# Sparse attention followed by a gated feed-forward on one core: fewer fillers and value sums first in the prologue; in unit 0 output products ahead of value products, and the last two pairs of x turned together, the last one copied by VectorE

## The chip, the core and the metric

The kernel runs on one core of a Trainium2 chip. The metric is the device time of one execution in microseconds (us); the median of several executions is quoted. The profile of one execution covers the span from its first to its last instruction, which is about 1.8 us shorter than the time.

## The reference

```python
# attention: q, k, v are [4, 8, 768, 64]
k_sum = k.reshape(B, H, nb, 32, D).max(axis=3)      # one key per block of 32
v_sum = v.reshape(B, H, nb, 32, D).mean(axis=3)     # one value per block
scores = concat(local scores within 16 positions, block scores + log(32))
x = softmax(scores) @ concat(v, v_sum)              # -> [3072, 512]
# gated feed-forward
h = gelu(x @ w_gate) * (x @ w_val)                  # 512 -> 1536
out = x + sigmoid(x @ w_res) * (h @ w_out)
```

## The kernel before

The work is cut into eight units of 384 rows. The heads go in four pairs. For a unit, TensorE makes scores `s`; ScalarE takes the exponential `P`; VectorE masks it; TensorE makes the value products `ao`; VectorE divides by the row sum (`xn`); the result is turned (`xp`, copied to `xT`). Then come twelve weight groups, numbered `fo` 0 to 11, each of one gate group `g` and one value group `vv` (four matmuls each). ScalarE takes gelu of `g`, and VectorE multiplies it by `vv` (`gvT`, called a product here). TensorE writes `g` and `vv` into four buffers of PSUM, its output memory. A later group can only start when ScalarE's gelu or VectorE's product has released its buffer; a semaphore, a counter that one engine raises and another waits for, tells it so. Slack is the time between such a release and the start that needs it. The output stage of a unit makes `r` (residual gate) and `f` (output products from `gvT` and `w_out`), and VectorE makes the residual steps `th` and `o`. The attention of the next unit is woven into this stage.

The first attention has nothing to hide behind; that is the prologue. Fillers (`keep_warm`) are matmuls on zeros whose result nobody reads; they keep TensorE busy.

```python
tq = [turn_pair(q_sb[0], hp, turn_tile(q_sb[0], ps_mm, "mm")) for hp in range(NP)]
for hp in range(3):
    q_place(0, hp, tq[hp])
keep_warm(1)
# ... scores of the four pairs, first value sums ...
vsum_mm(0, vs, 3, 8)
keep_warm(2)
# ...
for hp in range(3):
    av_first(hp, st, ao[hp], 0, BAND)       # own products of pairs 0..2
vsum_mm(0, vs, 8, 11)
av_first(3, st, ao[3], 0, BAND)             # own products of pair 3
vsum_mm(0, vs, 11, NT)
nc.vector.tensor_copy(vblk[...], vs[0][...])   # casts of the value sums
nc.scalar.copy(vblk[...], vs[1][...])
# ...
keep_warm(1)
for hp in range(4):
    av_first(hp, st, ao[hp], BAND, 128)     # products with the value sums
    av_end(hp, st, ao[hp])
keep_warm(3)
xt_step(0, 0, st, **turn[0])                # first turn of x
```

Unit 0's output stage, and two parts of the loop:

```python
def first_out(u, st, gvT, nst):
    # ...
    turn = dict(pool=ps_t, tag="t", copy=nc.scalar.copy)
    s_step(n, 0, nst)
    s_step(n, 1, nst, TO2)
    for sub in range(NSUB):
        res_step(st, sub)
    av_step(n, 0, nst)
    # ... see the diff

# loads, issued by GpSimd, in this order: w_gate and w_val in six chunks each,
# q_sb[1] ahead of the last chunk pair, w_res, then w_out in three chunks
for c in range(6):
    if c:
        load_w(w_gate, wg_src, c)
    load_w(w_val, wv_src, c)
    if c == 4:
        q_sb[1] = load_q(1, QJ)
nc.gpsimd.dma_start(out=w_res[:], in_=...)
for c in range(3):
    ...                                       # w_out

# unit 0: k, v and q of the second batch are asked for
load_k(nb, k_sb[nb], 0, 1)
v_loads(nb)
load_q_nat(nb)
# unit 1, after the weight groups fo = 0, 1, 2, 3: one pair of keys each on VectorE:
# a reduce over the block (L228) and three copies (L232, L236, L237)
if fo < NP:
    k_place(nb, fo, tk[fo])
```

The softmax here doesn't subtract the row's maximum and nothing guards it: scores larger than these inputs give would overflow.

Of the kernel before, what the change touches and what calls it, by code (L numbers as in the profile page):

```python
# [15 lines left out]
def kernel(  # L16
# [21 lines left out]
    FO = DFF // 128  # L38
    QT = 64
    NT = S // QT  # L40
    HT = NT // 2
    TU = S // 2
    NSUB = TU // 128
    NU = 2 * B
    NP = H // 2
    BAND = QT + 2 * WIN
# [14 lines left out]
    ps_o = ctx.enter_context(tc.tile_pool(name="ps_o", bufs=1, space=bass.MemoryType.PSUM))  # L61
# [73 lines left out]
    with tc.manual_schedule():  # L135
# [112 lines left out]
        def q_place(half, hp, tp):  # L248
            qj = q_sb[half].shape[2]
            nc.scalar.copy(qT[0][:, 3 * half:3 * half + 3, hp].rearrange("d c (p j) -> d c p j", j=qj),  # L250
                           tp.rearrange("d j (c p) -> d c p j", c=3))
# [10 lines left out]
        def vsum_mm(b, vs, lo, hi):  # L262
            for t in range(lo, hi):
                for i in range(2):
                    nc.tensor.matmul(vs[i][96:128, 0:DM // 2], bmat[:, t, :],
                                     vext[b % 2][0:QT, t, 4 * i:4 * i + 4, 0:D],
                                     start=(t == 0), stop=(t == NT - 1))
# [59 lines left out]
        def av_step(u, hp, st, pool=ps_o, tag="ao"):  # L327
            b, half = u // 2, u % 2
            P = st["P", hp]
            ao = pool.tile([128, NSUB, 2, D + 1], F32, tag=tag, name="ao")  # L330
            for sub in range(NSUB):
                for hh in range(2):
                    for e in range(2):
                        t = 2 * sub + e
                        nc.tensor.matmul(ao[64 * e:64 * e + 64, sub, hh, :], P[:, hh, t, :],  # L335
                                         vext[b % 2][:, half * HT + t, 2 * hp + hh, 0:D + 1],
                                         start=True, stop=True, skip_group_check=True)
            av_end(hp, st, ao)

        def av_first(hp, st, ao, lo, hi):  # L340
            P = st["P", hp]
            for sub in range(NSUB):
                for hh in range(2):
                    for e in range(2):
                        t, h = 2 * sub + e, 2 * hp + hh
                        rhs = vblk[lo:hi, h, :] if lo else vext[0][0:hi, t, h, 0:D + 1]
                        nc.tensor.matmul(ao[64 * e:64 * e + 64, sub, hh, :], P[lo:hi, hh, t, :], rhs,  # L347
                                         start=(lo == 0 and sub == 0 and hh == 0), stop=(lo > 0),
                                         skip_group_check=True)

        def av_end(hp, st, ao):
            rz = work.tile([128, NSUB, 2, 1], F32, tag="rz", name="rz")
            nc.vector.reciprocal(rz[:], ao[:, :, :, D:D + 1])
            xn = st["xn"][:, hp].rearrange("p s (h d) -> p s h d", d=D)
            nc.vector.tensor_mul(xn, ao[:, :, :, 0:D], rz.to_broadcast([128, NSUB, 2, D]))  # L355

        def xt_step(u, ko, st, pool, tag, copy=nc.vector.tensor_copy):
            xp = pool.tile([128, TU], BF16, tag=tag, name="xp")
            for sub in range(NSUB):
                nc.tensor.transpose(xp[:, sub * 128:(sub + 1) * 128],  # L360
                                    st["xn"][:, ko, sub, :], ident[:])
            copy(st["xT"][:, ko, :], xp[:])
# [5 lines left out]
        def new_unit():  # L368
            return {"xn": upool.tile([128, KO, NSUB, 128], BF16, tag="xn", name="xn"),
                    "xT": upool.tile([128, KO, TU], BF16, tag="xT", name="xT")}  # L370
# [12 lines left out]
        def mm_tile(name):  # L383
            return ps_mm.tile([128, 512], F32, tag="mm", name=name)
# [24 lines left out]
        def res_step(st, sub):  # L409
            ss = slice(sub * 128, (sub + 1) * 128)  # L410
            r = mm_tile("r")
            for ko in range(KO):
                nc.tensor.matmul(r[:], st["xT"][:, ko, ss], w_res[:, ko, :],  # L413
                                 start=(ko == 0), stop=(ko == KO - 1))
            st["th", sub] = work.tile([128, DM], F32, tag="th", name="th")
            nc.scalar.activation(st["th", sub][:], r[:], AF.Tanh, scale=0.5)  # L416

        def ffn_step(st, gvT, sub, lo, hi):
            ss = slice(sub * 128, (sub + 1) * 128)
            if lo == 0:  # L420
                st["f", sub] = mm_tile("f")
            for fo in range(lo, hi):
                nc.tensor.matmul(st["f", sub][:], gvT[:, fo, ss], w_out[:, fo, :],  # L423
                                 start=(fo == 0), stop=(fo == FO - 1), skip_group_check=True)
# [13 lines left out]
        def end_step(u, st, sub):  # L438
            end_part(u, st, sub, st["f", sub], slice(0, DM))
# [12 lines left out]
        def keep_warm(n):  # L452
            wp = ps_s.tile([128, 2, 512], F32, tag="s", name="wp")
            for _ in range(n):
                nc.tensor.matmul(wp[:, 0], warm[:, 0:128], warm[:], start=True, stop=True)  # L455
# [11 lines left out]
        tq = [turn_pair(q_sb[0], hp, turn_tile(q_sb[0], ps_mm, "mm")) for hp in range(NP)]  # L467
        for hp in range(3):
            q_place(0, hp, tq[hp])
        keep_warm(1)  # L470
        st = new_unit()
        vs = [ps_t.tile([128, 512], F32, tag="t", name="vs"), ps_o.tile([128, 512], F32, tag="ao", name="vs")]
        s_step(0, 0, st)
# [5 lines left out]
        s_step(0, 2, st)  # L479
        s_step(0, 3, st, MM2)  # L480
        vsum_mm(0, vs, 3, 8)
        keep_warm(2)
        gvT = upool.tile([128, FO, TU], BF16, tag="gvT", name="gvT")
        ao = [ps_mm.tile([128, NSUB, 2, D + 1], F32, tag="mm", name="ao") for _ in range(NP)]
        for hp in range(3):
            av_first(hp, st, ao[hp], 0, BAND)
        vsum_mm(0, vs, 8, 11)
        av_first(3, st, ao[3], 0, BAND)
        vsum_mm(0, vs, 11, NT)
        nc.vector.tensor_copy(vblk[96:128, 0:H // 2, 0:D],  # L490
                              vs[0][96:128, 0:DM // 2].rearrange("p (h d) -> p h d", d=D))
        nc.scalar.copy(vblk[96:128, H // 2:H, 0:D],
                       vs[1][96:128, 0:DM // 2].rearrange("p (h d) -> p h d", d=D))
        nc.scalar.activation(gate1[:], bias_t[0:1, :], AF.Gelu)
        keep_warm(1)
        for hp in range(4):
            av_first(hp, st, ao[hp], BAND, 128)
            av_end(hp, st, ao[hp])
        keep_warm(3)
        turn = [dict(pool=ps_t, tag="t", copy=nc.scalar.copy), dict(pool=ps_o, tag="ao", copy=nc.scalar.copy)]  # L500
        xt_step(0, 0, st, **turn[0])
        keep_warm(1)
# [39 lines left out]
        def first_out(u, st, gvT, nst):  # L542
            n = u + 1
            other = dict(pool=ps_t, tag="t")
            turn = dict(pool=ps_t, tag="t", copy=nc.scalar.copy)
            s_step(n, 0, nst)
            s_step(n, 1, nst, TO2)
            for sub in range(NSUB):
                res_step(st, sub)
            av_step(n, 0, nst)  # L550
            av_step(n, 1, nst, **other)
            s_step(n, 2, nst)
            for sub in range(NSUB):
                ffn_step(st, gvT, sub, 0, 4)
            xt_step(n, 0, nst, **turn)
            av_step(n, 2, nst)
            s_step(n, 3, nst)
            ffn_step(st, gvT, 0, 4, 8)
            ffn_step(st, gvT, 1, 4, 8)
            xt_step(n, 1, nst, **turn)  # L560
            ffn_step(st, gvT, 2, 4, 8)
            av_step(n, 3, nst)
            xt_step(n, 2, nst, **turn)
            ffn_step(st, gvT, 0, 8, FO)
            end_step(u, st, 0)
            ffn_step(st, gvT, 1, 8, FO)
            xt_step(n, 3, nst, **turn)
            ffn_step(st, gvT, 2, 8, FO)
            end_step(u, st, 1)
            end_step(u, st, 2)  # L570
# [40 lines left out]
        for u in range(NU):  # L611
# [7 lines left out]
            if u:  # L619
                gvT = upool.tile([128, FO, TU], BF16, tag="gvT", name="gvT")  # L620
# [42 lines left out]
            if u == NU - 1:  # L663
                last_out(u, st, gvT)
            else:
                nst = new_unit()
                (mid_out if u else first_out)(u, st, gvT, nst)
                st = nst
# [30 lines left out]
```

## Time and profile before

| | before |
|---|---|
| time, median of 3 | 257.49 us (257.44 to 257.61) |
| span of the profiled run | 255.7 us |
| TensorE busy | 97% |
| first matmul of unit 1 | 52.82 us |

From the page of the kernel before: the busy line, the TensorE clock and the DMA rate in forty slices of 6.4 us, and the chain of waits by engine.

```profile
PE 247.6 (97%) x2279; PEld 138.7 (54%) x2304; DVE 157.5 (62%) x349; ACT 127.4 (50%) x213; POOL 110.5 (43%) x155
...
PEclk9999999999999999999999999999999999999999
...
GB/s 80 178 142 174 197 202 207 189 167 164 134 40 87 169 114 140 126 142 169 131 11 94 174 110 157 108 150 154 130 15 73 141 0 3 50 138 0 0 3 123
...
PE 91%; ACT 3%; DMA 2%; DVE 2%; issue 1%; POOLq 0%; DVEq 0%
```

TensorE is busy all through, at full clock, and 91% of the chain that ended last is TensorE's. Slices five to eight (26 to 51 us) move about 200 GB/s: the weights are still coming in while unit 0 computes.

The timeline of TensorE in the prologue of before. Columns: start, length, engine, line, operation, output and inputs, active rows and columns, shape, count, and in brackets the idle time before and what ended it.

```profile
11.75 0.39 PE L455 MATMUL wp<-warm 128*128 128x512 bf16 x1
12.20 0.48 PE L292 MATMUL s<-ident,mneg 128*128 128x384 bf16 x2
...
16.20 0.39 PE L455 MATMUL wp<-warm 128*128 128x512 bf16 x1
16.74 0.76 PE L347 MATMUL ao<-vext,P 96*64 96x65 bf16 x36
...
18.49 0.39 PE L265 MATMUL vs<-vext,bmat 64*32 64x256 bf16 x2
...
19.30 0.95 PE L347 MATMUL ao<-vblk,P 32*64 32x65 bf16 x48
...
20.84 0.33 PE L360 MATMUL xp<-ident,xn 128*128 128x128 bf16 x3
```

A filler sits before the scores (12.20) and before the own products (16.74); the last value sums (18.49) stand behind pair 3's own products; the first turn is at 20.84.

TensorE late in unit 0 of before:

```profile
36.22 0.82 PE L375 MATMUL g<-xT,w_gate 128*128 128x384 bf16 x4
36.88 0.81 PE L375 MATMUL vv<-xT,w_val 128*128 128x384 bf16 x4
...
39.38 0.39 PE L413 MATMUL r<-w_res,xT 128*128 128x512 bf16 x1
```

No wait precedes these. A landing is the moment at which a transfer's completion reaches its semaphore in the trace. In this trace the last `w_val` chunk landed at 36.53, 0.35 us ahead of its use at 36.88, and `w_res` at 39.08, 0.30 us ahead of its use at 39.38.

VectorE where unit 0 ends and unit 1 begins (the seam), before:

```profile
50.30 0.56 DVE L355 TENSOR_TENSOR xn<-ao,rz 128x384 bf16<-128x384 f32 x1
51.13 0.69 DVE L429 SCALAR_TENSOR_TENSOR th<-th,f 128x512 f32<-128x512 f32 x1 [0.27 <-PE f L423]
...
55.11 0.55 DVE L381 TENSOR_TENSOR gvT<-ge,vv 128x384 bf16<-128x384 f32 x1
55.96 0.95 DVE L228 TENSOR_REDUCE ks<-kW 128x24 bf16<-128x768 bf16 x1 [0.30 <-ACT kW L243]
...
57.11 0.19 DVE L236 COPY kW<-kW 128x176 bf16<-128x176 bf16 x1
57.22 0.19 DVE L237 COPY kW<-kW 128x176 bf16<-128x176 bf16 x1
57.33 0.54 DVE L381 TENSOR_TENSOR gvT<-ge,vv 128x384 bf16<-128x384 f32 x1
```

```profile
54.44 5.31 POOL L123 DMA_DIRECT2D q_nat<-in_q_dram  x6
```

From 51.13 on VectorE runs with one rest of 0.30 us until 63.8: six residual steps, then products and key pairs in turn. TensorE meanwhile, before:

```profile
52.82 0.81 PE L375 MATMUL g<-xT,w_gate 128*128 128x384 bf16 x4
...
58.31 0.81 PE L375 MATMUL g<-xT,w_gate 128*128 128x384 bf16 x4
58.96 0.81 PE L375 MATMUL vv<-xT,w_val 128*128 128x384 bf16 x4
...
61.56 0.81 PE L375 MATMUL vv<-xT,w_val 128*128 128x384 bf16 x4
```

The groups follow each other at 0.65 us, without a gap.

### The profile page before, as it was taken

To read this page: it belongs to the slowest core of one execution; us is meant where nothing else is said; L and a number is where in the kernel's file an instruction comes from. 1 tells how busy PE (TensorE), PEld (TensorE's weight loads), DVE (VectorE), ACT (ScalarE), POOL (GpSimd) and SP (SyncE) were. 2 spreads that over 40 slices of the span, in tenths; PEclk is the share of its full clock that TensorE was granted. 3 is DMA by queue.
4 is the path that set the end of the run, shared out by engine and by line. 5 is a ranking of instruction groups with operands and counts; after the bars stand their busy time and mean duration, and the time that the engine had idled before them with its cause. 6 is when DMAs were issued, how large, how long until landed. Compare 5 with 4: busy or idle time off the path is not lost.

```text
span 255.7 us, 5810 instructions
## 1 busy us (share of the span) xinstructions
PE 247.6 (97%) x2279; PEld 138.7 (54%) x2304; DVE 157.5 (62%) x349; ACT 127.4 (50%) x213; POOL 110.5 (43%) x155
## 2 busy tenths in 40 slices
PE   7999999999999999999999999999999999999994
PEld 2566664565654565546654565545554565455544
DVE  5965776399367544767567544857567544854424
ACT  6666359366493338344482338244482337253320
POOL 8897542193334988265405986256404000000000
PEclk9999999999999999999999999999999999999999
DMA  5999999999923999979703999979803500240003
GB/s 80 178 142 174 197 202 207 189 167 164 134 40 87 169 114 140 126 142 169 131 11 94 174 110 157 108 150 154 130 15 73 141 0 3 50 138 0 0 3 123
DMA packets 98475, 29.34 MB, mean 115 GB/s; under 512 B 83592, under 2 KB 95312, under 8 KB 98352
## 3 DMA queue, kind: packets, MB, share of 16 engines
q0 software_dynamic: 68720, 14.76, 69.8%
q1 hardware_dynamic: 29728, 14.21, 25.6%
q8 instruction: 18, 0.29, 0.5%
q14 instruction: 9, 0.07, 0.2%
HBM read 29.36 MB, written 6.29 MB: 139 GB/s over the span
## 4 chain that ended last, share of the span: by engine, by line
PE 91%; ACT 3%; DMA 2%; DVE 2%; issue 1%; POOLq 0%; DVEq 0%
PE g L375 25%; PE vv L375 24%; PE f L423 23%; PE r L413 7%; PE ao L335 3%; PE s L299 2%; DMA k_sb<-in_k_dram 2%; PE tp L211 2%; PE wp L455 1%; ACT P L317 1%; PE vs L273 1%; PE ao L347 1%; ACT P L314 1%; DVE o L432 1%; DVE th L429 1%
## 5 line engine op out<-in xcount | busy, mean ns | idle before, releaser
L381 DVE TENSOR_TENSOR gvT<-ge,vv 128x384 bf16<-128x384 f32 x96 | 52.7, 552 | 51.2 <-PE vv L375 46.8
L380 ACT ACTIVATE ge<-g 128x384 f32<-128x384 f32 x96 | 47.0, 491 | 68.5 <-DVE gvT L381 38.0
L375 PE MATMUL g<-xT,w_gate 128*128 128x384 bf16 x384 | 78.8, 326 | 0.2
L375 PE MATMUL vv<-xT,w_val 128*128 128x384 bf16 x384 | 78.7, 326 | 0.0
L423 PE MATMUL f<-w_out,gvT 128*128 128x512 bf16 x262 | 62.7, 379 | 1.3 <-issue 1.0
L375 PEld LDWEIGHTS <-w_gate 128*128 128x128 bf16 x384 | 37.2, 98 | 26.5 <-issue 1.6
L375 PEld LDWEIGHTS <-w_val 128*128 128x128 bf16 x384 | 37.5, 98 | 24.8 <-issue 0.3
L423 PEld LDWEIGHTS <-gvT 128*128 128x128 bf16 x276 | 25.7, 98 | 29.2
L103 POOL DMA_DIRECT2D vext<-in_v_dram x48 | 33.0, 730 | 13.8 <-DMA w_out<-in_moe_w_out_dram 5.6
L416 ACT ACTIVATE th<-r 128x512 f32<-128x512 f32 x24 | 13.5, 607 | 27.5 <-PE r L413 27.5
L429 DVE SCALAR_TENSOR_TENSOR th<-th,f 128x512 f32<-128x512 f32 (+2 forms) x26 | 16.7, 641 | 14.2 <-PE f L423 14.2
L321 DVE TENSOR_TENSOR P<-P,maskt 128x768 bf16<-128x768 bf16 x30 | 16.9, 562 | 12.1 <-ACT P L317 6.6
L285 POOL COPY vext<-vsum 32x1536 bf16<-32x1536 bf16 x12 | 17.2, 1464 | 14.1 <-DMA vsum<-vpart 13.9
L413 PE MATMUL r<-w_res,xT 128*128 128x512 bf16 x88 | 22.7, 380 | 0.4
L432 DVE SCALAR_TENSOR_TENSOR o<-th,xn 128x512 f32<-128x512 f32 (+2 forms) x26 | 18.6, 715 | 0.9
L355 DVE TENSOR_TENSOR xn<-ao,rz 128x384 bf16<-128x384 f32 x32 | 17.8, 558 | 1.1
L317 ACT ACTIVATE P<-s,bias_t 128x768 bf16<-128x768 f32 x17 | 15.3, 903 | 4.3 <-PE s L299 4.1
L117 POOL DMA_DIRECT2D k_nat<-in_k_dram x24 | 16.5, 727 | 1.5 <-DMA k_nat<-in_k_dram 0.8
L123 POOL DMA_DIRECT2D q_nat<-in_q_dram x18 | 15.9, 917 | 0.7 <-issue 0.7
L314 ACT ACTIVATE P<-s,bias_t 128x384 bf16<-128x384 f32 x30 | 15.7, 581 | 0.0
L228 DVE TENSOR_REDUCE ks<-kW 128x24 bf16<-128x768 bf16 x16 | 15.1, 945 | 0.4 <-ACT kW L243 0.3
L413 PEld LDWEIGHTS <-xT 128*128 128x128 bf16 x96 | 8.8, 98 | 9.9
(82 smaller groups left out, 172.2 us busy)
## 6 DMA issues: line engine op xcount, KB each, us to landing
out_dram<-o SPq DMA_DIRECT2D x23, 256.0 KB, 2.3
vext<-in_v_dram POOLq DMA_DIRECT2D x48, 64.0 KB, 6.4
q_nat<-in_q_dram POOLq DMA_DIRECT2D x18, 128.0 KB, 7.2
w_gate<-in_moe_w_gate_dram POOLq DMA_DIRECT2D x6, 256.0 KB, 7.7
w_val<-in_moe_w_val_dram POOLq DMA_DIRECT2D x6, 256.0 KB, 8.3
w_out<-in_moe_w_out_dram POOLq DMA_DIRECT2D x3, 512.0 KB, 14.5
k_nat<-in_k_dram POOLq DMA_DIRECT2D x24, 64.0 KB, 4.7
vext<-vext SPq DMA_DIRECT2D x6, 144.0 KB, 5.4
```

Of the source, the lines that this page charges most:

```text
L103: nc.gpsimd.dma_start(out=vext[b % 2][0:QT, t, :, 0:D], in_=v[b, :, t * QT:(t + 1) * QT, :].rearrange("h p d -> p h d"))
L285: eng.tensor_copy(vext[b % 2][96:128, lo:hi, :, 0:D], src)
L314: nc.scalar.activation(P[:, hh].rearrange("p t q -> p (t q)"), s[hh][:, 0:TU], AF.Exp, scale=scale, bias=bias_t[:])
L317: nc.scalar.activation(P.rearrange("p a t q -> p a (t q)"), s2[:, :, 0:TU], AF.Exp, scale=scale, bias=bias_t[:])
L355: nc.vector.tensor_mul(xn, ao[:, :, :, 0:D], rz.to_broadcast([128, NSUB, 2, D]))
L375: nc.tensor.matmul(ps[:, 0:TU], w[:, ko, fo * 128:(fo + 1) * 128], st["xT"][:, ko, :], start=(ko == 0), stop=(ko == KO - 1), skip_group_ch ...
L380: nc.scalar.activation(ge[:], g[:, 0:TU], AF.Gelu)
L381: nc.vector.tensor_mul(gvT[:, fo, :], ge[:], vv[:, 0:TU])
L413: nc.tensor.matmul(r[:], st["xT"][:, ko, ss], w_res[:, ko, :], start=(ko == 0), stop=(ko == KO - 1))
L423: nc.tensor.matmul(st["f", sub][:], gvT[:, fo, ss], w_out[:, fo, :], start=(fo == 0), stop=(fo == FO - 1), skip_group_check=True)
L429: nc.vector.scalar_tensor_tensor(th[:, cs], th[:, cs], 1.0, f[:, 0:n], ALU.add, ALU.mult)
L432: nc.vector.scalar_tensor_tensor(o.rearrange("p (k d) -> p k d", d=128), th[:, cs].rearrange("p (k d) -> p k d", d=128), 0.5, x, ALU.mult, ...
```

## The change

Its intent: take fillers that stand in the way out of the prologue; finish the value sums sooner, so that their casts run while TensorE makes pair 3's own products; in unit 0's output stage cover the waits for the masked `P` by output products; and turn the last two pairs of x one after the other, the fourth with its copy on VectorE (the default of `xt_step`) instead of ScalarE.

```diff
         for hp in range(3):
             q_place(0, hp, tq[hp])
-        keep_warm(1)
         st = new_unit()
 ...
         vsum_mm(0, vs, 3, 8)
-        keep_warm(2)
+        keep_warm(1)
 ...
         for hp in range(3):
             av_first(hp, st, ao[hp], 0, BAND)
-        vsum_mm(0, vs, 8, 11)
-        av_first(3, st, ao[3], 0, BAND)
-        vsum_mm(0, vs, 11, NT)
+        vsum_mm(0, vs, 8, NT)
 ...
         nc.scalar.activation(gate1[:], bias_t[0:1, :], AF.Gelu)
+        av_first(3, st, ao[3], 0, BAND)
         keep_warm(1)
         for hp in range(4):
             av_first(hp, st, ao[hp], BAND, 128)
             av_end(hp, st, ao[hp])
-        keep_warm(3)
+        keep_warm(1)
 ...
             for sub in range(NSUB):
                 res_step(st, sub)
+            ffn_step(st, gvT, 0, 0, 4)
             av_step(n, 0, nst)
             av_step(n, 1, nst, **other)
             s_step(n, 2, nst)
-            for sub in range(NSUB):
-                ffn_step(st, gvT, sub, 0, 4)
+            ffn_step(st, gvT, 1, 0, 4)
+            ffn_step(st, gvT, 2, 0, 4)
+            ffn_step(st, gvT, 0, 4, 8)
             xt_step(n, 0, nst, **turn)
             av_step(n, 2, nst)
             s_step(n, 3, nst)
-            ffn_step(st, gvT, 0, 4, 8)
             ffn_step(st, gvT, 1, 4, 8)
+            ffn_step(st, gvT, 2, 4, 8)
+            ffn_step(st, gvT, 0, 8, FO)
             xt_step(n, 1, nst, **turn)
-            ffn_step(st, gvT, 2, 4, 8)
             av_step(n, 3, nst)
+            ffn_step(st, gvT, 1, 8, FO)
             xt_step(n, 2, nst, **turn)
-            ffn_step(st, gvT, 0, 8, FO)
+            xt_step(n, 3, nst, ps_o, "ao")
             end_step(u, st, 0)
-            ffn_step(st, gvT, 1, 8, FO)
-            xt_step(n, 3, nst, **turn)
             ffn_step(st, gvT, 2, 8, FO)
```

## The prediction

> **What bounds the kernel.** TensorE: the page has PE busy 97% of a 255.7 us span at granted clock 1.0; the chain of waits is PE 91%. Outside the start-up and unit 0's output stage the chain is gapless. So the change can act only before about 63 us.
>
> **Prologue.** By the timeline: one filler (11.75) sits before the first scores (12.20); ScalarE then idles 0.41 us before the first exp (13.01). Two fillers (16.20) precede the own products (16.74). The last value sums start at 18.49, after pair 3's own products; the vblk casts they release start at 18.81, the value products at 19.30. Three fillers delay the first turn of x to 20.84, though xn was done at 20.50.
> One 128x512 filler occupies 0.216 us, plus about 0.1 to 0.2 at the change of tile. Expected: first exp 0.4 earlier; own products only 0.2 earlier, because value tile 7 lands at 15.86 and its sum (15.90) holds the queue; casts 0.6 earlier, value products 0.5, first turn 0.7; from the second turn about 0.5 (VectorE's reciprocal and multiply, 0.7 us per pair, sets it).
>
> **Given back to DMA.** The weights come at DMA pace, about 200 GB/s in the slice table, whatever PE does. Landings: last w_val chunk 36.53 (used 36.88), w_res 39.08 (used 39.38), w_out chunks 41.65, 44.18, 46.71. So of 0.5 us about 0.25 survives: r starts near 39.14.
>
> **Unit 0's output stage** (38.92 to 52.82). Four output products ahead of the value products cover the waits for masked P (0.09 and 0.19 us). Fewer changes of operation and no gap at 49.3 save another 0.2 or so. w_out arrives just in time (41.65 against 41.74). Unit 1's first gate matmul should start near 52.1 instead of 52.82.
>
> **But VectorE pays.** The fourth turn's copy moves from ScalarE (0.48 us) to VectorE, ahead of the first residual step; VectorE executes in order (the Trainium skill, "TensorE: Matmul & The Clock Gate", opening table: a strict FIFO; the timeline agrees). Before, the residual steps start at 51.13 and VectorE runs almost without rest to 63.78: six steps to 55.11, first product, 0.30 idle, then four k pairs and products at 1.82 us each. After: fourth turn at 51.05, copy 51.4 to 51.9, residual steps from about 51.9, first reduce at 56.35 instead of 55.96. PE's sixth value matmul group of unit 1 (61.56) starts 0.06 us after the fourth product releases its PSUM buffer (61.50): no slack. I estimate it at 61.95. So PE's 0.7 us is lost and about 0.4 more; everything later shifts by +0.4.
>
> **Clock.** The skill (same page, closing table) warns of PE idle above about 3 us. Removing fillers leaves gaps under 0.7 us; the clock stays 1.0.
>
> **Prediction.** 257.8 us, range 257.0 to 258.3. Faster by over 2%: 0.01; within 2%: 0.98; slower: 0.01.
>
> **Signs.** Right: r near 39.1; first gate matmul of unit 1 near 52.1; VectorE's first residual step near 51.9; new PE waits for gvT multiplies at 58 to 62; unit 1's score stage (70.97) 0.1 to 0.5 later. Wrong: residual steps starting by 51.3, or no PE wait in 56 to 62: then about 0.7 us is gained (256.8). If r starts at 38.9 or earlier, landings are not fixed as I assume.
>
> **What would make it wrong.** Weights landing differently; the VectorE copy cheaper or earlier; the later units absorbing the shift.

## The result, and the profile after

A ratio here is the mean time of one kernel's fast runs over the mean of the other's fast runs of the same rounds, so it is not quite the ratio of the medians that are quoted.

| | before | changed |
|---|---|---|
| time, median of 6 | 257.45 us (257.37 to 257.61) | 257.20 us (256.80 to 257.28) |
| ratio | | 0.9987, 95% interval 0.9974 to 1.0 |
| span of the profiled run | 255.7 us | 255.5 us |

The same within 2%, and 0.25 us faster at the median; the interval just reaches no change. A second measurement (`changed_again` below) gave 0.9978, interval 0.9960 to 0.9996. It was run at another time.

From the page of the changed kernel, the busy line and the chain by engine:

```profile
PE 246.8 (97%) x2277; PEld 138.2 (54%) x2300; DVE 157.9 (62%) x350; ACT 126.9 (50%) x212; POOL 110.5 (43%) x155
...
PE 80%; DMA 10%; DVE 4%; POOL 3%; issue 2%; POOLq 0%; DVEq 0%
```

TensorE's share of the chain fell from 91% to 80%; DMA came in with 10% and VectorE rose from 2% to 4%. The total hardly moved, but the path of the waits has. The 10% is the length of the transfers that the chain runs over, not time lost to them: the wait for the longest of them, below, is 0.40 us.

TensorE in the prologue, changed:

```profile
11.68 0.50 PE L292 MATMUL s<-ident,mneg 128*128 128x384 bf16 x2
...
16.41 0.76 PE L347 MATMUL ao<-vext,P 96*64 96x65 bf16 x36
17.10 1.04 PE L265 MATMUL vs<-vext,bmat 64*32 64x256 bf16 x8
...
18.70 0.96 PE L347 MATMUL ao<-vblk,P 32*64 32x65 bf16 x48
...
19.96 0.34 PE L360 MATMUL xp<-ident,xn 128*128 128x128 bf16 x3
```

Against before: scores 0.52 earlier, own products 0.33, value products 0.60, first turn 0.88. The third weight group started at 24.26 instead of 24.92, a lead of 0.66 us.

TensorE late in unit 0, changed:

```profile
35.55 0.82 PE L375 MATMUL g<-xT,w_gate 128*128 128x384 bf16 x4
36.61 0.82 PE L375 MATMUL vv<-xT,w_val 128*128 128x384 bf16 x4 [0.23 <-DMA w_val<-in_moe_w_val_dram]
...
39.13 0.82 PE L413 MATMUL r<-w_res,xT 128*128 128x512 bf16 x2
```

The value group should follow its gate group by 0.66 us, as it did before (36.22 to 36.88). It follows by 1.06: it waits 0.40 for the last `w_val` chunk (the bracket counts only the idle after the modelled end of the matmul before). Of the lead 0.25 us is left at `r`.

VectorE at the seam, changed:

```profile
51.50 0.36 DVE L362 COPY xT<-xp 128x384 bf16<-128x384 bf16 x1 [0.45 <-PE xp L360]
51.78 0.68 DVE L429 SCALAR_TENSOR_TENSOR th<-th,f 128x512 f32<-128x512 f32 x1
...
56.21 0.95 DVE L228 TENSOR_REDUCE ks<-kW 128x24 bf16<-128x768 bf16 x1
...
57.34 0.71 DVE L236 COPY kW<-kW 128x176 bf16<-128x176 bf16 x1
57.46 0.63 DVE L237 COPY kW<-kW 128x176 bf16<-128x176 bf16 x1
58.02 0.53 DVE L381 TENSOR_TENSOR gvT<-ge,vv 128x384 bf16<-128x384 f32 x1
```

The new copy stands ahead of the residual steps, which start 0.65 later (51.78 against 51.13). The rest before the reduce is used up, so the reduce is 0.25 later. Then something that the diff does not touch: the two small copies of the first key pair take 0.71 and 0.63 instead of 0.19 each. They overlap, so the loss is about 0.45, and the second product of unit 1 is 0.69 later than before (58.02 against 57.33). The six q loads of the second batch are issued by GpSimd as before (there from 54.44 on), one every 0.87 us:

```profile
54.46 5.30 POOL L123 DMA_DIRECT2D q_nat<-in_q_dram  x6
```

TensorE meanwhile, changed:

```profile
52.16 0.81 PE L375 MATMUL g<-xT,w_gate 128*128 128x384 bf16 x4
...
57.65 0.81 PE L375 MATMUL g<-xT,w_gate 128*128 128x384 bf16 x4
58.60 0.81 PE L375 MATMUL vv<-xT,w_val 128*128 128x384 bf16 x4
...
61.20 0.81 PE L375 MATMUL vv<-xT,w_val 128*128 128x384 bf16 x4
```

Unit 1 starts 0.66 earlier than before (52.16 against 52.82): the output stage gained 0.41. The fourth value group follows its gate group by 0.95 instead of 0.65, so it waits 0.30. Its first matmul waits on VectorE's semaphore, and the product that started at 58.02 ends at 58.55. One more wait of 0.12 stands before the gate group at 64.14. 0.66 - 0.30 - 0.12 = 0.24 us remain and stay to the end. (In the trace of `changed_again` 0.44 stayed: `r` had started 0.22 earlier there, and the waits were alike.)

The same in the chain of the changed kernel, in order of time (start, length, what):

```profile
24.95 11.62 DMA w_val<-in_moe_w_val_dram
...
57.34 0.71 DVE kW L236
...
58.09 0.47 DVE gvT L381
...
58.60 0.81 PE vv L375 x4
```

The chain runs over the transfer of the last `w_val` chunk (issued at 24.95, landed 11.62 later), and later over the slow copy and the product into the fourth value group.

### The profile page after: what moved, and what is told of

Read it like the earlier page. It is cut to its first block, busy times and chain, and to the rows that moved or that the text cites. A ratio compares the mean times of both kernels' runs of the same rounds, so it can differ in the third digit from the quotient of the medians.

```text
span 255.5 us, 5803 instructions
## 1 busy us (share of the span) xinstructions
PE 246.8 (97%) x2277; PEld 138.2 (54%) x2300; DVE 157.9 (62%) x350; ACT 126.9 (50%) x212; POOL 110.5 (43%) x155
## 4 chain that ended last, share of the span: by engine, by line
PE 80%; DMA 10%; DVE 4%; POOL 3%; issue 2%; POOLq 0%; DVEq 0%
PE f L423 23%; PE vv L375 21%; PE g L375 21%; PE r L413 8%; DMA w_val<-in_moe_w_val_dram 5%; DMA w_gate<-in_moe_w_gate_dram 3%; PE ao L335 3%; DMA q_sb<-in_q_dram 3%; PE s L299 3%; POOL vext L103 1%; DVE th L429 1%; DVE o L432 1%; PE vs L273 1%; POOL w_val L161 1%; POOL w_gate L161 1%
```

## The experiments

All outputs are right. Some expectations speak of "r in unit 2": the `r` at about 71 us is meant, in unit 1's output stage. It is the same point throughout. This table holds the readings of the profiled runs; "r to r" is the time between the first `r` matmuls of units 0 and 1, so it is free of what happened before 39 us. For the kernels with cut transfers the landing is that of the second half of the chunk.

| kernel | last w_val landed | first r | r to r | waits for VectorE in unit 1 | ratio to before (95%) |
|---|---|---|---|---|---|
| before | 36.53 | 39.38 | 32.05 | 0 | 1 |
| changed | 36.56 | 39.13 | 32.06 | 0.30 + 0.12 | 0.9987 (0.9974 to 1.0) |
| changed_again | 36.33 | 38.91 | 32.07 | 0.32 + 0.13 | 0.9978 (0.9960 to 0.9996) |
| prologue_only | 36.46 | 39.02 | 32.05 | 0 | 0.9981 (0.9967 to 0.9995) |
| output_only | 36.66 | 39.33 | 31.84 | 0.18 + 0.03 | 0.9981 (0.9969 to 0.9994) |
| copy_on_scalar | 36.70 | 39.26 | 31.72 | 0.09 | 0.9970 (0.9958 to 0.9983) |
| copy_again | 36.93 | 39.49 | 31.64 | 0 | 0.9982 (0.9969 to 0.9995) |
| one_filler_back | 36.06 | 39.05 | 31.89 | 0 | 0.9991 (0.9978 to 1.0005) |
| three_fillers_back | 36.20 | 39.47 | 31.64 | 0 | 0.9985 (0.9972 to 0.9997) |
| split_loads | 36.23 | 38.83 | 31.72 | 0 | 0.9964 (0.9947 to 0.9982) |
| split_again | 37.00 | 39.23 | 31.64 | 0 | 0.9958 (0.9944 to 0.9971) |
| split_spread | 36.42 | 38.80 | 31.64 | 0 | 0.9962 (0.9941 to 0.9982) |
| spread_only | 37.25 | 39.84 | 31.74 | 0 | 0.9985 (0.9966 to 1.0004) |

Ratios of different calls have intervals that overlap widely; only the largest differences among them are settled by time. The traces are what tells the theories apart.

### prologue_only

The edit: the first four hunks of the diff alone, the output stage as before.

> The kernel before with the prologue part alone (fewer fillers, value sums ahead of pair 3's own products). Theory (the weight transfers set a floor): the third weight group starts about 0.6 us earlier than in before (24.3 against 24.92), the value group of fo 10 waits for the last w_val chunk (lands near 36.55) and starts near 36.61, r starts near 39.13, so 0.25 us of the 0.6 is left; the output stage keeps it, no new wait for VectorE in unit 1: 257.2, 0.25 faster than before. Rival 1 (what the prologue gains is gained): 0.6 faster, 256.85. Rival 2 (the prologue's gain is all lost later to the VectorE chain): same as before, 257.45.

Measured: 257.16 (256.86 to 257.56) against 257.60 of before, ratio 0.9981. The third weight group started at 24.32, 0.60 earlier than before; the value group of `fo` 10 waited 0.24 and started at 36.50, 0.04 after its chunk landed; `r` started at 39.02. No wait followed, and r to r was that of before. So the prologue gains 0.60 us on TensorE, the wait for the weights takes back 0.24, and 0.36 is left at `r`. Rival 1 falls in the trace; rival 2 falls too, since what is left at `r` stays. The time alone does not tell them apart: its interval runs from 0.13 to 0.85 us faster.

### output_only

The edit: the last hunk alone.

> The kernel before with unit 0's output stage alone in the new order. Theory: r starts at 39.38 as in before; TensorE finishes the stage about 0.4 us earlier (first gate group of unit 1 near 52.4 against 52.82), but the first residual step of VectorE starts near 52.0 instead of 51.13, the fourth value group of unit 1 then waits for VectorE (near 58.85) and another group later (near 64.4), and nothing is left: 257.45, within 0.1 of before. Rival (TensorE's own order decides): 0.4 faster, 257.05.

Measured: 257.19 (257.16 to 257.29), ratio 0.9981. The expectation of "nothing left" was wrong: both waits came where expected (58.68 and 64.12) but took 0.18 and 0.03. r to r is 31.84, 0.21 better than before. Only one copy of the first key pair (L232) was slow in this run (0.61 instead of 0.24), where the changed kernel had two at 0.71 and 0.63. That pointed at the slow copies. The new output stage alone shortened the time from the first `r` to the first gate group of unit 1 from 13.44 to 13.04 us; which of its moves brings how much was not tried.

### copy_on_scalar and copy_again

The edit, against the changed kernel:

```diff
-            xt_step(n, 3, nst, ps_o, "ao")
+            xt_step(n, 3, nst, ps_o, "ao", nc.scalar.copy)
```

> The changed kernel with one word altered: the copy of the fourth turned pair goes back to ScalarE, the turns stay together. Theory (the copy ahead of the residual steps on VectorE costs what the output stage gained): the first residual step starts near 51.1 instead of 51.78, TensorE has no wait for VectorE at the fourth value group of unit 1 nor after, the lead of 0.66 us at the first gate group is kept to the end: 256.8, 0.4 faster than the changed kernel and 0.65 faster than before. Rival (the four k pairs of 1.8 us each bound VectorE in any case, wherever the residual steps start): the wait stays, within 0.1 of the changed kernel, 257.2.

Measured: 256.97 (256.64 to 257.29), ratio 0.9970. The residual steps started at 51.10. The waits shrank from 0.42 to 0.09, and r to r fell from 32.06 to 31.72. Two of the small copies were slow here too (0.70 and 0.62), but they came 0.68 earlier, and of the waits only 0.09 before the fifth value group (59.82) was left. `r` itself started later than in the changed kernel's run, since the last chunk landed later (36.70).

> The changed kernel with the fourth copy on ScalarE, again, as the control for split_again on the same chip: 256.85, about 0.7 faster than before; from r in unit 0 to r in unit 2 31.7 us (32.06 in the changed kernel).

Measured: 257.06 (256.96 to 257.71), ratio 0.9982, so 0.2 us short of the expectation. r to r was 31.64 as expected, with no wait. But the last chunk landed at 36.93, and the value group waited 0.61 for it, so `r` started at 39.49. The word in the diff is worth 0.34 to 0.42 us in r to r in both traces; the times do not settle it, because the landings move by as much.

### one_filler_back and three_fillers_back

The edit, with `n` of 1 or 3, against the changed kernel:

```diff
             if fo == 2:
+                keep_warm(n)
                 vext_consts(1)
```

> The changed kernel with one filler of 0.216 us put between two weight groups of unit 0 (after fo 2), where TensorE has no gap. Theory: the wait of 0.40 us before the value group of fo 10 shrinks by what the filler costs, r starts at 39.13 as before it, and the time is that of the changed kernel within 0.05: 257.2. Rival (TensorE's work in unit 0 is on the path): 0.2 to 0.3 slower, 257.45.

Measured: 257.60 (257.03 to 257.83), ratio 0.9991. In the trace `r` started at 39.05 as the theory said, but in that run the chunk had landed early, at 36.06, so no wait was left to absorb the filler; a wait of 0.24 for the first `w_out` chunk (landed at 41.85) followed instead. The times spread over 0.8 us and lean to the rival, and the profiled run was the fastest of the five (257.03). Inconclusive. The trace shows one thing more: the moved copy was in place (residual steps from 51.96), no key copy took over 0.32, and the fourth value group started without a wait at 58.48, after the second product had ended at 58.31.

> The changed kernel with three fillers (0.65 us) after fo 2 of unit 0. Theory: 0.25 to 0.4 of it vanishes in the wait before the value group of fo 10, which is gone, the rest shows: r starts near 39.4, the time is 0.25 to 0.4 above the changed kernel, 257.5. Rival (the work of TensorE in unit 0 is all on the path): 0.65 above it, 257.8.

Measured: 257.20 (257.18 to 257.50), ratio 0.9985. `r` started at 39.47, 0.34 later than in the changed kernel's trace and 0.56 later than in `changed_again`'s. Yet the time is that of the changed kernel within its noise, lower than the expected 257.5. In the trace r to r is 31.64 and no wait for VectorE is left. Two waits stand one behind the other, and work put ahead of them fills both. That 0.65 us of empty matmuls cost so little speaks against the rival of a fully exposed TensorE.

### changed_again

The changed kernel, unedited.

> The changed kernel again, as the control of this chip: about 0.3 us faster than before (257.2 against 257.5), a wait of 0.2 to 0.4 us of TensorE for VectorE at the fourth value group of unit 1, and a wait before the value group of fo 10 of unit 0 that ends with the landing of the last w_val chunk.

Measured: 257.04 (256.94 to 257.43), ratio 0.9978. The waits of 0.32 and 0.13 and both slow copies (0.73 and 0.66) came again, at almost the same places; the wait for the last chunk was 0.09 here, since it landed at 36.33.

### split_loads and split_again

The edit, against copy_on_scalar: the same bytes in the same order, in more transfers.

```diff
-            load_w(w_val, wv_src, c)
+            if c < 5:
+                load_w(w_val, wv_src, c)
+            else:
+                for i in range(2):
+                    nc.gpsimd.dma_start(out=w_val[:, 2 * i:2 * i + 2, c * 256:],
+                                        in_=wv_src[:, 2 * i:2 * i + 2, c * 256:])
 ...
-        nc.gpsimd.dma_start(out=w_res[:], in_=...)
+        for i in range(KO):
+            nc.gpsimd.dma_start(out=w_res[:, i:i + 1], in_=wr_src[:, i:i + 1])
 ...
-        for c in range(3):
-            sl = slice(c * 4, (c + 1) * 4)
+        for lo, hi in ((0, 2), (2, 4), (4, 8), (8, 12)):
+            sl = slice(lo, hi)
```

> The changed kernel with the fourth copy on ScalarE and the late weight transfers cut into pieces (last w_val chunk into two halves by contraction chunk, w_res into four, the first w_out chunk into two), same bytes in the same order. Theory (whole-transfer landings are the floor in unit 0): the value group of fo 10 starts without waiting for the whole chunk, r starts near 38.8 instead of 39.2, the first output product does not wait, and the prologue's 0.6 us is kept: 0.3 faster than copy_on_scalar, 1.0 faster than before (256.5). Rival (the bytes or the issue rate are the floor, the number of pieces does not matter): no faster than copy_on_scalar, 256.85, or slower.

Measured: 256.77 (256.59 to 256.96), ratio 0.9964, 0.35 us below `changed_again` on the same chip (means of five, 256.75 and 257.10). `r` started at 38.83 as expected. The timeline of TensorE late in unit 0 in split_loads:

```profile
35.67 0.82 PE L381 MATMUL g<-xT,w_gate 128*128 128x384 bf16 x4
36.33 0.81 PE L381 MATMUL vv<-xT,w_val 128*128 128x384 bf16 x4
...
38.83 1.04 PE L419 MATMUL r<-w_res,xT 128*128 128x512 bf16 x4
```

The value group follows its gate group by 0.66, without a wait. But the whole chunk had landed at 36.23 in this run, so this trace alone does not show that the halves were needed. Hence the repeat beside its control:

> split_loads again, beside copy_again on one chip. Theory (landings of whole transfers hold TensorE in unit 0): r starts at most at 38.85 and does not move with the landings, where copy_again waits for the last w_val chunk and starts r between 39.0 and 39.3; from r to r 31.7 in both; so 0.2 to 0.4 faster than copy_again and closer together from run to run. Rival (pieces do not matter): within 0.1 of copy_again.

Measured: 256.59 (256.54 to 256.97), ratio 0.9958, 0.54 us below `copy_again` on the same chip (means 256.67 and 257.21), more than the 0.2 to 0.4 expected. In this profile the second half landed at 37.00, after the group had begun at 36.73, and no wait appeared; the same group in copy_again:

```profile
36.97 0.82 PE L375 MATMUL vv<-xT,w_val 128*128 128x384 bf16 x4 [0.45 <-DMA w_val<-in_moe_w_val_dram]
```

`r` started at 39.23, not at 38.85 as I had said: the wait had moved to the chunk before, still whole, which landed at 33.17 and held its group for 0.27. It landed late in this run; in the others it came at 31.80 to 32.38 and held nothing, except in spread_only, where nothing was cut (33.50, a wait of 0.70). So where a whole chunk lands after its group could start, its landing holds the group; that cutting one chunk delays the one before is not shown. Which of the three cuts does how much was not tried.

### split_spread and spread_only

The edit, against split_loads and against the changed kernel:

```diff
-                        if fo < NP:
-                            k_place(nb, fo, tk[fo])
+                        if fo in (0, 2, 3, 5):
+                            i = (0, 2, 3, 5).index(fo)
+                            k_place(nb, i, tk[i])
```

> As split_loads, and the four k pairs of unit 1 are placed after fo 0, 2, 3 and 5 instead of 0, 1, 2 and 3, so that VectorE gets time between them. Theory: only the small wait left in copy_on_scalar (0.08 us near 59.8) goes, so within 0.1 of split_loads; if VectorE still binds there, 0.2 to 0.3 faster than it. Rival: the later placing delays the keys that unit 1's score stage needs, slower.

Measured: 256.56 (256.52 to 257.08), ratio 0.9962: that of split_loads (means 256.65 and 256.75), as expected. With the copy on ScalarE nothing is left to relieve.

> The changed kernel (copy still on VectorE ahead of the residual steps) with the four k pairs of unit 1 after fo 0, 2, 3 and 5. Theory (the backlog of VectorE from the residual steps plus the k pairs is what takes back the output stage's gain): with a pair less between the first products the fourth value group no longer waits and the gain is kept, 256.85, 0.3 to 0.4 faster than changed_again. Rival (the delay comes from something else than VectorE's backlog): no change.

Measured: 257.30 (256.96 to 257.69), ratio 0.9985; the time missed the expectation, and is not below `changed_again` (means 257.28 and 257.10). The trace says that the mechanism was right and hidden: no wait for VectorE, r to r 31.74 against 32.07. But in the profiled run the weights came late (`w_res` at 39.80), and `r` started at 39.84, 0.93 after `changed_again`'s. The edit touches unit 1 only, so I take this to be the scatter of the landings; the other runs have no trace.

### q_loads_late

The edit, against the changed kernel: the q loads of the second batch are taken from their place in unit 0 and put into unit 1.

```diff
                 v_loads(nb)
-                load_q_nat(nb)
 ...
+                    if nb == 1 and fo == 4:
+                        pool_after(gvT[0:1, 3, 0:1])
+                        load_q_nat(nb)
```

> The changed kernel with the six q loads of the second batch issued by GpSimd only after the fourth product of unit 1 (about 62.5) instead of at 54.5 to 59.8. It is slower as a whole, by several us, since unit 2 waits for q; the stage at 55 to 63 is what it is for. Theory (the VectorE copies of 0.6 to 0.7 us at the first k pair are slowed by GpSimd's writing of DMA descriptors at the same time): no copy of the key pairs takes over 0.3 us, the second product starts near 57.5 instead of 58.0, and TensorE does not wait at the fourth value group. Rival (they are slow for another reason, such as the start order): the slow copies and the wait of 0.3 us stay.

Measured: one look, 263.79, clock 0.986 over the run, state unknown; 6 us slower, as was meant, because unit 2 waits for q. Only the stage at 55 to 63 us is read. VectorE there:

```profile
57.52 0.20 DVE L236 COPY kW<-kW 128x176 bf16<-128x176 bf16 x1
57.64 0.19 DVE L237 COPY kW<-kW 128x176 bf16<-128x176 bf16 x1
57.75 0.54 DVE L381 TENSOR_TENSOR gvT<-ge,vv 128x384 bf16<-128x384 f32 x1
```

And TensorE's fourth value group, which follows the gate group at 57.83 by 0.65:

```profile
58.48 0.81 PE L375 MATMUL vv<-xT,w_val 128*128 128x384 bf16 x4
```

The small copies take their usual 0.19 to 0.20, and TensorE does not wait at all between 52 and 66 us, although the residual steps start at 51.95, as late as in the changed kernel. The only key copy over 0.3 us (0.32 at 62.82) comes after the q loads have resumed at 62.22. So the slow copies come from GpSimd's issuing of loads at the same time, and without them the moved copy alone brings no wait. That it is the writing of descriptors within the issue, as the expectation has it, no run shows.

The kept traces say when a copy is slow. In the fourteen of them, 79 key copies of unit 1 fell into the time in which the six q loads were issued. Measured from the start of the load instruction before it:

| copy began, us after the start of the load instruction | copies | their length | they ended, after that start |
|---|---|---|---|
| 0 to 0.24 or over 0.73 | 51 | 0.14 to 0.24 | |
| 0.26 to 0.70 | 23 | 0.32 to 0.71 | 0.92 to 1.03 |

Five fell between these bounds, some slow and some not. The first pair's two small copies began 0.05 and 0.16 us after a load instruction in before, and 0.27 and 0.39 after one in the changed kernel; the load itself began at 57.06 and 57.07. So the delay of 0.25 from the moved copy pushed them from the harmless part of an issue into the slow one.

Two cautions. q_loads_late is one look, though the trace of one_filler_back agrees with it. And unit 1 starts at 52.34 here, so TensorE had 0.18 us less lead to lose; but the second product ended at 58.29, 0.19 before the group began, so the 0.18 would just have fitted. In one_filler_back it is the same to 0.02: unit 1 starts at 52.35, and 0.17 was left.

## Why the prediction was right or wrong, point by point

- **What bounds the kernel, and where the change can act: right.** After 71 us the two traces differ by a shift only.
- **The prologue: right, a little under.** Predicted and measured, in us earlier than before: first exponential 0.4 and 0.50, own products 0.2 and 0.33, casts 0.6 and 0.74, value products 0.5 and 0.60, first turn 0.7 and 0.88. About 0.1 of each is the earlier arrival of the inputs in that run (the turns of q began 0.07 earlier, the value sum that waits for its tile 0.12).
- **Given back to DMA: right.** `r` was predicted near 39.14 and came at 39.13. The last `w_val` chunk was the one that bound; `w_res` then landed 0.04 ahead of its use. prologue_only and split_again show the wait as the cause. That the prediction hit to 0.01 us is luck: it took the landings as fixed, and in `changed_again` `r` came at 38.91.
- **The output stage: right.** Unit 1's first gate group was predicted near 52.1 and came at 52.16. `w_out` was just in time (landed at 41.62, used at 41.73).
- **VectorE's delay: right at the start.** Residual steps near 51.9, measured 51.78; first reduce 56.35, measured 56.21. The cause is the in-order execution that the prediction took from the Trainium skill, "TensorE: Matmul & The Clock Gate", opening table: VectorE reached the residual steps only after the copy, although the output products that the first one needs were finished at 49.68.
- **What this costs TensorE: wrong.** The step that failed is "PE's sixth value matmul group of unit 1 (61.56) starts 0.06 us after the fourth product releases its PSUM buffer (61.50): no slack". The two times stand side by side by chance. I had assumed that buffers go round in order. In the changed trace the sixth group starts at 61.20, while the fourth product starts only at 61.73; its first matmul waits on ScalarE's semaphore, not VectorE's, and so it does in before's trace. The binding buffer was at the fourth group, which waits for the second product. Before, that product ended at 57.87 and the group started at 58.96: a slack of 1.09 us where I had counted none. So TensorE lost 0.42, where I had put the lead of 0.7 and 0.4 more, and a gain of 0.24 stayed where I had forecast a loss of 0.4. One thing more in the semaphores: the fifth value group waits on VectorE's in before (it started at 60.26, 0.58 after the third product had ended at 59.68) and on ScalarE's in the changed kernel. The two programs hand out the buffers differently, so a slack read from one does not carry over whole to the other.
- **A term that was missing.** VectorE's delay at the second product, 0.69, is 0.25 from the moved copy (0.65 later, less the idle that it uses up) and about 0.45 from the slow key copies, which that 0.25 had brought into the slow part of a load issue. Of the 1.09 us of slack TensorE's lead uses 0.66; the delay of 0.25 alone would still fit. q_loads_late and one_filler_back show it: without copies slowed by more than about 0.1 us there is no wait. copy_on_scalar shows the other half: with the slow copies, but without the moved copy, 0.09 of waiting. The whole wait of 0.42 takes both.
- **Clock: right.** The closing table of the same page warns of idle over about 3 us; the gaps that removing fillers left were below 0.7 us, and the clock stayed at 1.0.
- **The time:** 257.8 was forecast and 257.2 came, inside the range of 257.0 to 258.3, but the sign of the small change was wrong, for the reason of the sixth group. The range held both signs, so that the time fell into it says little for the mechanism. The score stage at the end of unit 1 came at 70.73, 0.24 earlier than before (70.97), where 0.1 to 0.5 later was forecast.
- **Left open:** what within a load issue holds up a copy that begins in its later part. (Before and prologue_only had no copy over 0.3 us in that stage, though q loads were being issued there too, because their copies fell outside that part; the table under q_loads_late has the bounds.) Also open is what moves the landings of the weights by up to 1.2 us (36.06 to 37.25 for the last chunk) from run to run.

The best of the kernels run are the three with cut transfers and the copy on ScalarE: ratios 0.9958 to 0.9964 to before, and the two that ran beside the changed kernel are 0.35 and 0.45 us below it (means of five). They beat both.

## What to carry to other kernels

Time that a saving frees is spent at the next wait in line, so list the slack at each point where the saved engine meets another one, and do it with the semaphore that is really waited on, not with two times that happen to agree. Where a whole transfer lands late, as the last `w_val` chunk did here, its landing holds also the matmuls that need only its first piece; try cutting the transfers that arrive last. Before moving a copy to the engine with the lower load, look at what stands behind it in that engine's order, and at what else slows that engine at that moment, as the loads that GpSimd issued did here.

## What the Trainium skill lacked or had wrong

- "SBUF — State Buffer", section "Who interferes with whom", says that VectorE copies in its two-port modes and GpSimd exclude each other fully, and that `tensor_reduce` never contends. The traces fit this, though none shows the mode of a copy: the small key copies went from 0.19 to between 0.63 and 0.73 us in the changed kernel's two runs with loads being issued by GpSimd, the reduce beside them stayed at 0.94 to 0.95, and with the loads moved away the copies were 0.19 to 0.20. The page's own worked case is a copy that holds up descriptors. For the reverse seen here it has a bare ratio (a measurement of "DVE 6.8× slower") and no time; here it was about 0.45 us per hit with loads issued every 0.87 us. No page that I found says which part of a load issue holds up a copy: here it was copies that began 0.26 to 0.70 us after its start.
- "TensorE: Matmul & The Clock Gate", section "Back-to-back issue gap", gives about 131 ns per matmul at N=512 as the sustained spacing of weight loads and matmuls. Here the same stream ran at 216 ns: in before's chain 24 `f` matmuls of 128x512 take 5.19 us. At N=384 the step was 162.5 ns. Both fit the formula that the section gives for the isolated gap, N/2.4 + 2.5 ns, and elsewhere the page has 216 ns as the back-to-back gap at N=512 too.
- No page that I read says how much the landing of one load varies between runs of the same program on one core: the last `w_val` chunk landed between 36.06 and 37.25 us in the runs that did not cut it, and an experiment of 0.3 us on this kernel was drowned by it more than once.
